# The MLP's first product, 512 columns at a time or 256

## The chip, the cores and the metric

The kernel runs on one NeuronCore of a Trainium2 chip. The metric is the device time of one execution in microseconds (us). Its engines run programs of their own and meet through semaphores: TensorE (PE in the profile, with its weight loads in a row of their own, PEld), VectorE (DVE), ScalarE (ACT), GpSimd (POOL) and SyncE (SP), which here only issues DMAs.

## The reference

Sliding-window attention over 8 batches, 8 heads, 576 positions and 64 features per head, followed by a two-layer MLP over the 4608 tokens:

```
scores = (q @ k^T) / sqrt(64) + alibi bias, masked to 0 <= i - j < 128
attn   = softmax(scores)
x      = (attn @ v), heads joined: 4608 tokens x 512
h      = x @ w_in                      # 512 -> 2048
g      = 0.5 * h * (1 + erf(h / sqrt(2)))
out    = g @ w_out                     # 2048 -> 512
```

Everything is float32 at the interface. The kernel reaches that accuracy with pairs of 16-bit numbers: a value is split into a high and a low half, and a product of two such values is the sum of three 16-bit products (high by high, low by high, high by low).

## The kernel before

**Tiles.** The 4608 tokens are nine tiles of 512, t = 0 to 8. Tile t is finished by attention over batches t and t - 1, since a batch has 576 tokens. Attention goes by units, (b, hp): a batch and one of four pairs of heads. A unit has scores (`sc`, L394), `s` with the bias (L416), a softmax into `e_main` (exponentials on ACT, the high half on POOL at L489, the low half on DVE at L143), a transposing DMA `et<-e_main` in two pieces (L492), and the product `av` with v (L529). The head pair hp of `av` becomes 128 of the 512 features of `x`: ACT writes the high half (L542), DVE the low half (`low_part`, L143).

**The MLP.** `mlp_in(t, fc)` (L566) makes one of 16 blocks of 128 features of h: 12 matrix products add up in one bank of PSUM, `ph`, named h{t}_{fc}. They go over the four groups of input features, cc (which are the head pairs of x), and for each over the three pairs of halves; the third of them reads the low half of x. The stationary operand is a 128x128 block of `wi`, and each product loads its own. A GELU on ACT (L586 in tile 0, L589 after it) empties the bank, and POOL and DVE split the result into halves (L590, L143). There are four banks for h and the output products together (tag "mm"), four for scores and av (tag "att"), and three buffers for the GELU's float32 result (tag "ob"). `mlp_out` (L601, products at L608 in tile 0 and at L611 after it) is the second layer; its 512 columns are the output features.

**Stages.** In tile 0 the weights are turned into halves on DVE and ACT while the first MLP runs; this is the time up to about 210 us, with the four units of batch 1 in its last third. From then on the loop at L721 runs through tiles 1 to 8: 16 blocks of h, then 16 groups of output products, with the scores and av of the next batch put between them. For tiles 7 and 8 there is no attention left to mix in. `split_qk(b)` (L340) takes the largest absolute value of q and of k (`stq`), makes scales from them (`scq`) and splits both into `qbuf` and `kbuf`.

**What sets the order.** The program is written in the order of these loops, and a scheduler with a model of the engines puts the instructions of each engine in the order in which its model finds them ready, priorities first. Each engine, and the queue of SP, then runs its list strictly in that order. An instruction that is not ready holds up all that stand behind it on its engine. Two calls raise priorities by 400 instructions: the exponentials (`EXP_AHEAD`), and the first product of tile 0 (L682).

Of the kernel before, what the change touches and what calls it, by code (L numbers as in the profile page):

```python
# [19 lines left out]
P = 128  # L20
# [4 lines left out]
NCC, NFC = DM // P, DFF // P  # L25
NT = B * S
TT = 512
# [25 lines left out]
def attention_gelu_mlp(  # L53
# [10 lines left out]
    nc = tc.nc  # L64
# [77 lines left out]
    def low_part(dst, src, scale, high):  # L142
        nc.vector.scalar_tensor_tensor(  # L143
            out=dst, in0=src, scalar=scale, in1=high, op0=ALU.mult, op1=ALU.subtract
        )
# [64 lines left out]
    wi, wo, zo = [], {}, []  # L210
# [68 lines left out]
    def x_tile(t):  # L279
        if t not in xt:  # L280
            xt[t] = pool.tile([P, NCC, 2, TT], F16, tag="x", name=f"x{t}", bufs=2)
        return xt[t]
# [283 lines left out]
    def mlp_in(t, fc):  # L566
        n, k = divmod(fc, 2)
        ph = psum.tile([P, TT], F32, tag="mm", name=f"h{t}_{fc}", bufs=4)
        x = x_tile(t)
        i = 0  # L570
        for cc in range(NCC):
            for a, b in ((0, 0), (1, 0), (0, 1)):
                nc.tensor.matmul(  # L573
                    ph, wi[n][:, a, cc, k * P : (k + 1) * P], x[:, cc, b, :],
                    start=(i == 0), stop=(i == 3 * NCC - 1),
                )
                i += 1
        q, r = divmod(fc, 4)
        if r == 0:
            if t == 0:  # L580
                g_of[t, q] = pool.tile([P, 4, TT], F32, tag="g", name=f"g{t}_{q}", bufs=4)
            else:
                g_of[t, q] = pool.tile([P, 4, 2, TT], F16, tag="g", name=f"g{t}_{q}", bufs=4)
        g = g_of[t, q]
        if t == 0:
            nc.scalar.activation(g[:, r], ph, AF.Gelu, scale=gsc[t, n])  # L586
            return
        g32 = pool.tile([P, TT], F32, tag="ob", name=f"g32_{t}_{fc}", bufs=3)
        nc.scalar.activation(g32, ph, AF.Gelu, scale=gsc[t, n])  # L589
        nc.gpsimd.tensor_scalar(g[:, r, 0], g32, gsg[t, n], 1.0, op0=ALU.mult, op1=ALU.mult)  # L590
        low_part(g[:, r, 1], g32, gsg[t, n], g[:, r, 0])
# [86 lines left out]
    for n in range(NWP):  # L678
        if n == 2:
            load_qk(1)  # L680
        with tc.high_priority(400):
            tile_scales(0, [n])  # L682
            for k in range(2):
                mlp_in(0, 2 * n + k)
        if n == 3:
            stat_v(1)
            split_qk(1)
            split_v(1)
            load_v(2)
        if n == 5:  # L690
            stat_v(2)
        weights_out_raw(n)
        fetch(1)
# [27 lines left out]
    for t in range(1, NTILE):  # L721
        b = t + 1
# [4 lines left out]
        for step in range(2 * NFC):  # L727
            if step < NFC:
                mlp_in(t, step)
            else:  # L730
                tb, q = divmod(step - NFC, 4)
                for fc in range(4 * q, 4 * q + 4):
                    mlp_out(t, tb, fc)
            if b >= B:
                continue
            if step in at:
                hp, i = at[step]
# [56 lines left out]
```

## Time and profile before

| | us |
|---|---|
| three runs | 956.73, 960.18, 960.32 (median 960.18) |
| the profiled execution, its own time | 963.32 |
| its span, first to last instruction | 961.4 |
| PE busy | 922.8 |
| DVE busy | 643.7 |
| ACT busy | 436.6 |
| POOL busy | 255.8 |

The profiled execution lies 3.14 us above the median of the three runs, and 1.9 us of its time lie outside the span. The durations below are those of the profiled execution. In a row of the profile, `L573 PE MATMUL h<-x,wi 128*128 128x512 f16 x1728 | 386.7, 382 | ...` reads: line 573, engine, operation, what is written from what, the part of the array, the shape of the moving operand, the count; then busy time in us and the mean duration of one in ns. Matrix products are pipelined, so that the mean duration of one (382 ns) is longer than the distance from one to the next. A row of the timeline begins with start and length in us, and ends with the idle time ahead of it and what ended it, in brackets. `A:B` rows give the busy time of each engine within a stretch, with its count of instructions, the granted share of the TensorE clock, and what the DMA engines did.

### The profile page before, as it was taken

To read this page: it belongs to the slowest core of one execution; us is meant where nothing else is said; L and a number is where in the kernel's file an instruction comes from. 1 tells how busy PE (TensorE), PEld (TensorE's weight loads), DVE (VectorE), ACT (ScalarE), POOL (GpSimd) and SP (SyncE) were. 2 spreads that over 40 slices of the span, in tenths; PEclk is the share of its full clock that TensorE was granted. 3 is DMA by queue.
4 is the path that set the end of the run, shared out by engine and by line. 5 is a ranking of instruction groups with operands and counts; after the bars stand their busy time and mean duration, and the time that the engine had idled before them with its cause. 6 is when DMAs were issued, how large, how long until landed. Compare 5 with 4: busy or idle time off the path is not lost. (4 is left out here: it accounts for less than half of the span.)

```text
span 961.4 us, 17491 instructions
## 1 busy us (share of the span) xinstructions
PE 922.8 (96%) x6996; PEld 446.1 (46%) x6996; DVE 643.7 (67%) x1270; ACT 436.6 (45%) x943; POOL 255.8 (27%) x516
## 2 busy tenths in 40 slices
PE   7988999769999899999999999999999999999998
PEld 3553444334454345444544444444544454444443
DVE  6699999989985877688767876777566632201300
ACT  6565445545553565256526653564465413201200
POOL 1010103324441433144313530363144312201200
PEclk9789999989999999999999999999999999999999
DMA  9525742972466224713372357244313430000000
GB/s 320 201 69 167 235 137 39 217 201 60 84 130 157 50 50 80 206 40 61 85 194 49 59 94 171 56 78 83 79 25 57 83 73 12 1 22 23 1 12 33
DMA packets 172451, 91.18 MB, mean 95 GB/s; under 512 B 132561, under 2 KB 153169, under 8 KB 172241
## 3 DMA queue, kind: packets, MB, share of 16 engines
q1 hardware_dynamic: 172368, 90.06, 37.9%
q8 instruction: 55, 0.90, 0.4%
q14 instruction: 28, 0.22, 0.1%
HBM read 46.53 MB, written 9.44 MB: 58 GB/s over the span
## 5 line engine op out<-in xcount | busy, mean ns | idle before, releaser
L573 PE MATMUL h<-x,wi 128*128 128x512 f16 x1728 | 386.7, 382 | 9.6 <-ACT g L589 3.9
L573 PEld LDWEIGHTS <-wi 128*128 128x128 f16 x1728 | 166.6, 98 | 212.4 <-issue 14.0
L611 PE MATMUL o<-wo,g 128*128 128x512 f16 x1152 | 259.9, 379 | 0.0
L611 PEld LDWEIGHTS <-g 128*128 128x128 f16 x1536 | 145.9, 98 | 174.3
L590 POOL TENSOR_SCALAR g<-g,sg 128x512 f16<-128x512 f32 x128 | 100.1, 786 | 288.7 <-ACT g L589 281.7
L143 DVE SCALAR_TENSOR_TENSOR g<-g,sg,g 128x512 f16<-128x512 f32 x128 | 106.2, 843 | 92.0 <-POOL g L590 92.0
L483 ACT ACTIVATE s<-s,nmax 128x192 f32<-128x192 f32 x252 | 111.2, 443 | 107.7 <-DVE nmax L480 105.0
L489 POOL TENSOR_SCALAR e_main<-s,z 128x192 f16<-128x192 f32 x252 | 124.3, 511 | 114.9 <-issue 37.3
L589 ACT ACTIVATE g<-h,gs 128x512 f32<-128x512 f32 x128 | 85.9, 687 | 137.3 <-PE h L573 108.5
L143 DVE SCALAR_TENSOR_TENSOR e_main<-s,z,e_main 128x192 f16<-128x192 f32 x252 | 112.1, 487 | 11.1 <-POOL e_main L489 10.8
L611 PE MATMUL o<-wo_first,g 128*128 128x512 f16 x384 | 88.2, 379 | 0.0
L394 PE MATMUL sc<-kbuf,qbuf 64*64 64x192 f16 (+1 forms) x1656 | 77.6, 266 | 9.4 <-DMA kbuf<-kp 4.4
L416 DVE SCALAR_TENSOR_TENSOR s<-sc,cs,bias_h 128x384 f32<-128x384 f32 x112 | 63.9, 606 | 15.1 <-PE sc L394 14.9
L542 ACT ACTIVATE x<-av,cx 128x448 f16<-128x448 f32 (+6 forms) x52 | 23.9, 477 | 86.0 <-PE av L529 85.8
L480 DVE TENSOR_REDUCE nmax<-s 128x5 f32<-128x960 f32 (+1 forms) x56 | 58.5, 1044 | 2.2
L608 PE MATMUL o<-zo,g 128*128 128x512 f32 x128 | 57.0, 598 | 0.0
L529 PE MATMUL av<-et,vbuf 128*64 128x128 f16 (+1 forms) x1680 | 45.2, 213 | 11.4 <-DMA et<-e_main 10.3
L421 POOL MEMSET s<- 64x128 f32 (+1 forms) x112 | 19.6, 176 | 134.5 <-DVE s L416 133.7
L619 ACT ACTIVATE ob<-o,so 128x512 f32<-128x512 f32 x16 | 10.9, 679 | 96.9 <-PE o L611 96.8
L394 PEld LDWEIGHTS <-qbuf 64*64 64x64 f16 x1512 | 35.2, 106 | 42.0 <-issue 39.4
L529 PEld LDWEIGHTS <-vbuf 128*64 128x64 f16 x1680 | 42.2, 113 | 21.3 <-issue 19.5
L621 DVE TENSOR_SCALAR ob<-o,so 128x512 f32<-128x512 f32 x16 | 11.9, 744 | 60.0 <-PE o L611 60.0
(128 smaller groups left out, 715.1 us busy)
## 6 DMA issues: line engine op xcount, KB each, us to landing
v<-vp SPq DMA_DIRECT2D x32, 320.0 KB, 5.0
out<-ob SPq DMA_DIRECT2D x36, 256.0 KB, 2.1
raw<-w_in SPq DMA_DIRECT2D x8, 1024.0 KB, 14.1
raw<-w_out SPq DMA_DIRECT2D x8, 1024.0 KB, 5.0
q<-qp SPq DMA_DIRECT2D x7, 1152.0 KB, 6.1
k<-kp SPq DMA_DIRECT2D x7, 1152.0 KB, 6.3
qbuf<-qp SPq DMA_DIRECT2D x4, 288.0 KB, 4.5
kbuf<-kp SPq DMA_DIRECT2D x4, 288.0 KB, 4.9
```

Of the source, the lines that this page charges most:

```text
L143: nc.vector.scalar_tensor_tensor(out=dst, in0=src, scalar=scale, in1=high, op0=ALU.mult, op1=ALU.subtract)
L394: nc.tensor.matmul(ps[bank][o, n, 0:W], a, m, start=(i == 0), stop=(i == len(terms) - 1 and b > 0), skip_group_check=True,)
L416: nc.vector.scalar_tensor_tensor(out=s[:, bank[0] : bank[0] + k, :], in0=ps[bank][:, 0:k, 0:W], scalar=cs, in1=bias.broadcast_to([P, k, W] ...
L480: nc.vector.tensor_reduce(out=nmax[:, r], in_=s[:, r], axis=AX.X, op=ALU.max, negate=True)
L483: nc.scalar.activation(s[:, i, :], s[:, i, :], AF.Exp, bias=nmax[:, i : i + 1], accum_out=z[:, i : i + 1])
L489: nc.gpsimd.tensor_scalar(e[:, i, 0, c], s[:, i], z[:, i : i + 1], 1.0, op0=ALU.mult, op1=ALU.mult)
L529: nc.tensor.matmul(av[r, (j - blocks[0]) * QB : (j - blocks[0] + len(js)) * QB], v32s[b][:, hp, kb, r] if b < EXACT else vbuf[:, vi, hp, k ...
L573: nc.tensor.matmul(ph, wi[n][:, a, cc, k * P : (k + 1) * P], x[:, cc, b, :], start=(i == 0), stop=(i == 3 * NCC - 1),)
L589: nc.scalar.activation(g32, ph, AF.Gelu, scale=gsc[t, n])
L590: nc.gpsimd.tensor_scalar(g[:, r, 0], g32, gsg[t, n], 1.0, op0=ALU.mult, op1=ALU.mult)
L608: nc.tensor.matmul(o, g[:, r, c], zo[n][:, n % 2, k * DM : (k + 1) * DM], start=(fc == 0), stop=(fc == NFC - 1))
L611: nc.tensor.matmul(o, g[:, r, a, c], wo[n][:, b, k, :], start=(fc == 0 and i == 0), stop=(fc == NFC - 1 and i == 2),)
```

## The change

Each block of features of h is now made in two halves of 256 tokens. First 12 products fill the left half of the bank, then 12 more, with the same 12 stationary blocks loaded again, fill the right half. The GELU still reads the whole bank at once. `skip_group_check=True` tells the checker that two accumulations live in a bank.

```
-        i = 0
-        for cc in range(NCC):
-            for a, b in ((0, 0), (1, 0), (0, 1)):
-                nc.tensor.matmul(
-                    ph, wi[n][:, a, cc, k * P : (k + 1) * P], x[:, cc, b, :],
-                    start=(i == 0), stop=(i == 3 * NCC - 1),
-                )
-                i += 1
+        for c in (slice(0, TT // 2), slice(TT // 2, TT)):
+            i = 0
+            for cc in range(NCC):
+                for a, b in ((0, 0), (1, 0), (0, 1)):
+                    nc.tensor.matmul(
+                        ph[:, c], wi[n][:, a, cc, k * P : (k + 1) * P], x[:, cc, b, c],
+                        start=(i == 0), stop=(i == 3 * NCC - 1), skip_group_check=True,
+                    )
+                    i += 1
```

The 1728 products of L573 and their 1728 weight loads become 3456 of each (at L574). Later lines move down by one. Because the scheduler counts and models instructions, the lists of the other engines change too. From tile 2 on DVE, ACT, POOL and SP differ only by neighbours that change places; the larger differences lie in tile 0 and at the start of tile 1. PE differs also at the openings of tiles 2 and 3, in the same way as shown here for tile 1: the last av of tile 2 has nine half products of h_0 ahead of it in place of nine whole ones.

**PE, the opening of tile 1.** The blocks h_0 to h_3 of tile 1 are worked on while the last head pairs of batch 1 come in. Before, at the point where the low half of the last head pair's x is there, one product of each of the four blocks is left (`sc_0` are scores of batch 2):

```order
L394 MATMUL sc_0_2_2171<-kbuf,qbuf 64x192
L573 LDWEIGHTS wi_635
L573 MATMUL h_0_1970<-x_1107,wi_635 128x512
L573 LDWEIGHTS wi_635
L573 MATMUL h_1_1988<-x_1107,wi_635 128x512
L573 LDWEIGHTS wi_638
L573 MATMUL h_2_2016<-x_1107,wi_638 128x512
L573 LDWEIGHTS wi_638
L573 MATMUL h_3_2033<-x_1107,wi_638 128x512
L394 LDWEIGHTS qbuf
L394 MATMUL sc_0_4_2217<-kbuf,qbuf 64x192
```

Now, at the same point, h_0 goes on from its left half into its right half; the list has 13 products of h_0 here, then 13 of h_1, of h_2 and of h_3, and then h_4:

```order
L394 MATMUL sc_0_2_2471<-kbuf,qbuf 64x192
L574 LDWEIGHTS wi_635
L574 MATMUL h_0_2162<-x_1299,wi_635 128x256
L574 LDWEIGHTS wi_635
L574 MATMUL h_0_2162<-x_1299,wi_635 128x256
```

In the whole list no right half begins ahead of the end of its left half. So 44 of the 48 products of 512 columns stood ahead of this point, and now 44 of the 96 of 256 columns do.

**SP, the transposing DMAs of batch 1's units** (`et_1` to `et_3` are the units hp 1 to 3, two pieces each; `k_2` is the k of batch 2, `wo_first` a copy of a weight tile). Before:

```order
L492 DMA_TRANSPOSE et_1_1288<-e_main 128x20x128
L622 DMA out<-ob_0_1830 128x512
L273 DMA wo_first<-wo_1735 128x4096
L622 DMA out<-ob_2_1838 128x512
L492 DMA_TRANSPOSE et_1_1288<-e_main 128x16x128
L492 DMA_TRANSPOSE et_2_1415<-e_main 128x20x128
L622 DMA out<-ob_1_1834 128x512
L622 DMA out<-ob_3_1842 128x512
L337 DMA k_2_1930<-kp 128x4x576
L492 DMA_TRANSPOSE et_2_1415<-e_main 128x16x128
L492 DMA_TRANSPOSE et_3_1611<-e_main 128x20x128
```

Now:

```order
L492 DMA_TRANSPOSE et_1_1480<-e_main 128x20x128
L492 DMA_TRANSPOSE et_1_1480<-e_main 128x16x128
L492 DMA_TRANSPOSE et_2_1607<-e_main 128x20x128
L623 DMA out<-ob_0_2022 128x512
L623 DMA out<-ob_1_2026 128x512
L623 DMA out<-ob_2_2030 128x512
L273 DMA wo_first<-wo_1927 128x4096
L623 DMA out<-ob_3_2034 128x512
L492 DMA_TRANSPOSE et_2_1607<-e_main 128x16x128
L337 DMA k_2_2122<-kp 128x4x576
L492 DMA_TRANSPOSE et_3_1803<-e_main 128x20x128
```

The second piece of et_1 and the first of et_2 have moved ahead of the weight copy, and the load of k_2 behind the second piece of et_2.

**DVE, the end of unit (1, 3).** Before, the maximum of k_2 (`stq`) stands between the fourth and the fifth of the nine low halves of `e_main` of this unit:

```order
L143 SCALAR_TENSOR_TENSOR e_main<-s_3_1540,z_3_1610,e_main 128x192 x2
L208 TENSOR_REDUCE stq_1933<-k_2_1930 128x1
L143 SCALAR_TENSOR_TENSOR e_main<-s_3_1540,z_3_1610,e_main 128x192 x2
L113 COPY quarters<-stq_1933 32x2
L143 SCALAR_TENSOR_TENSOR e_main<-s_3_1540,z_3_1610,e_main 128x192
```

Now it stands behind all nine of them, and behind the low half of x of head pair 2:

```order
L143 SCALAR_TENSOR_TENSOR e_main<-s_3_1732,z_3_1802,e_main 128x192 x3
L143 SCALAR_TENSOR_TENSOR x_1299<-av_2_1_1940,cx_1_979,x_1299 128x448
L143 SCALAR_TENSOR_TENSOR e_main<-s_3_1732,z_3_1802,e_main 128x192
L143 SCALAR_TENSOR_TENSOR x_1721<-av_2_2_1985,cx_2_1155,x_1721 128x128
L208 TENSOR_REDUCE stq_2125<-k_2_2122 128x1
```

The steps behind it are in the same order as before: the scales, `qbuf`, `kbuf`, and only then the low half of x of head pair 3.

## The prediction

> **What bounds the kernel now.** I read the page's busy shares first, then busy time by stretches, then PE's timeline where it has gaps.
>
> ```profile
> PE 922.8 (96%) x6996; PEld 446.1 (46%) x6996; DVE 643.7 (67%) x1270; ACT 436.6 (45%) x943; POOL 255.8 (27%) x516
> L573 PE MATMUL h<-x,wi 128*128 128x512 f16 x1728 | 386.7, 382 | 9.6 <-ACT g L589 3.9
> L573 PEld LDWEIGHTS <-wi 128*128 128x128 f16 x1728 | 166.6, 98 | 212.4 <-issue 14.0
> ...
> core 0: us, PE busy (x) PEld busy (x) DVE busy (x) ACT busy (x) POOL busy (x), PEclk, DMA share, GB/s
> 60.00:130.00 70.00, 66.00 (x289) 30.78 (x288) 69.54 (x97) 35.37 (x42) 7.31 (x4) 1.00 0.55 178
> ...
> 195.00:200.00 5.00, 4.20 (x70) 3.31 (x71) 4.93 (x14) 1.00 (x2) 1.82 (x4) 0.50 0.39 65
> ...
> 215.00:250.00 35.00, 35.00 (x228) 15.84 (x227) 33.95 (x77) 19.23 (x37) 15.77 (x26) 1.00 0.32 69
> ```
>
> PE is busy for 96% of the span, but not everywhere alone: from 60 to 130 us DVE is full (69.54 of 70 us) and PE is not. From 215 us on PE has no idle time (35.00 of 35), and after that it only stops for a few waits. So an addition to h's products in tile 0 should vanish behind DVE, and one in tiles 1 to 8 should count in full. What matters is the distance between products, not the 382 ns that one lasts.
>
> **What a half product costs.** The rows are of PE's timeline (a run in tile 7, a run of float32 products, a run of av) and PEld's:
>
> ```profile
> 819.76 8.58 PE L573 MATMUL h<-x,wi 128*128 128x512 f16 x39
> ...
> 819.98 8.08 PEld L573 LDWEIGHTS <-wi 128*128 128x128 f16 x38
> ...
> 110.70 19.48 PE L608 MATMUL o<-zo,g 128*128 128x512 f32 x45
> ...
> 494.81 0.78 PEld L529 LDWEIGHTS <-vbuf 128*64 128x64 f16 x26
> ...
> L529 PEld LDWEIGHTS <-vbuf 128*64 128x64 f16 x1680 | 42.2, 113 | 21.3 <-issue 19.5
> L608 PE MATMUL o<-zo,g 128*128 128x512 f32 x128 | 57.0, 598 | 0.0
> ```
>
> 39 products take 8.58 us with the last one's 0.38 us: (8.58 - 0.38) / 38 = 215.8 ns apart. The float32 products of the same shape are (19.48 - 0.60) / 44 = 429.1 ns apart, twice as long within 2.5 ns. If float32 streams its columns twice, then columns cost 213.3 ns per 512 and each product a fixed 2.5 ns. A product of 256 columns then takes 106.7 + 2.5 = 109.1 ns, a pair 218.3, which is **2.5 ns more for each old product**. The bounds: 0 if the 2.5 ns goes with columns, and the whole weight load of 98 ns if the load no longer hides. A load starts with the product ahead of it (the run of loads begins one distance, 0.22 us, into the run of products). It has 109 ns for 98. And in av, 26 loads, 13 for each half of the array's columns, run in 0.78 us, one each 56 ns or so, though a load's row says 113 ns. So the load's duration isn't its pace, and I take 2.5 ns. A rule of the Trainium skill speaks against it: "TensorE: Matmul & The Clock Gate", Part 3 (Packing small matmuls, The mechanism), says that weight loads overlap products in flight only when they go to other rows of the array. By that rule 1728 more loads would stand on the path. The trace disagrees: the 38 loads above go to the same 128 rows as the products among which they run, and the products are no further apart for it.
>
> In tiles 2 to 8 there are 7 x 16 x 12 = 1344 old products: 1344 x 2.5 ns = **+3.3 us**, all on PE's path. Tile 0's 192 would add 0.5 us, which lies behind DVE. GELUs also change places with other work of ACT in tile 0. One example is h_9's GELU, now behind a weight step that waits for its DMA. I price that at nothing, because PE has waits enough behind it, the next rows.
>
> **The opening of tile 1.** This is PE's timeline from the end of batch 1's scores, then DVE's and SP's around it:
>
> ```profile
> 178.46 0.69 PE L394 MATMUL sc<-kbuf,qbuf 64*64 64x192 f16 x23 [3.43 <-DVE s L416]
> ...
> 188.32 2.75 PE L573 MATMUL h<-x,wi 128*128 128x512 f16 x12 [1.80 <-ACT x L542]
> 195.72 2.77 PE L529 MATMUL av<-et,vbuf 128*64 128x128 f16 x66 [4.64 <-DMA et<-e_main]
> 198.57 3.47 PE L573 MATMUL h<-x,wi 128*128 128x512 f16 x12
> 205.26 1.60 PE L529 MATMUL av<-et,vbuf 128*64 128x128 f16 x66 [3.22 <-DMA et<-e_main]
> ...
> 209.81 1.02 PE L573 MATMUL h<-x,wi 128*128 128x512 f16 x4
> ...
> 211.78 7.93 PE L573 MATMUL h<-x,wi 128*128 128x512 f16 x36 [0.58 <-ACT g L589]
> ...
> 190.71 0.57 DVE L143 SCALAR_TENSOR_TENSOR e_main<-s,z,e_main 128x192 f16<-128x192 f32 x1 [0.62 <-POOL e_main L489]
> ...
> 193.78 2.55 DVE L208 TENSOR_REDUCE stq<-k 128x1 f32<-128x2304 f32 x1 [1.01 <-DMA k<-kp]
> ...
> 204.01 2.62 DVE L143 SCALAR_TENSOR_TENSOR qbuf<-q,scq,qbuf 128x2304 f16<-128x2304 f32 x1 [2.17 <-ACT qbuf L351]
> 206.55 2.61 DVE L143 SCALAR_TENSOR_TENSOR kbuf<-k,scq,kbuf 128x2304 f16<-128x2304 f32 x1
> 209.08 0.68 DVE L143 SCALAR_TENSOR_TENSOR x<-av,cx,x 128x448 f16<-128x448 f32 x1
> ...
> 187.16 0.39 SPq L337 DMA_DIRECT2D k<-kp  x1
> ```
>
> PE waits here again and again for the last head pairs, and fills the time with 44 of the 48 products of h_0 to h_3. The last 4 start at 209.81, when the low half of the last x is there (DVE, 209.08 + 0.68). Call that time T. From T on PE works without a stop but for 0.58 us in which it waits for the first GELU to free a bank.
>
> Now a right half cannot begin ahead of its left half's end, so only 44 of 96 half products stand ahead of T, 4.8 us of cover where 9.5 were. Left behind T: before, 4 + 12 x 12 = 148 products, 31.9 us; now 52 + 12 x 24 = 340 half products, 37.1 us. That is 5.2 us more. The 0.58 us go, because 48 half products run while the first GELU works. **+4.6 us**, if T stays. This has tile 1's own 2.5 ns per product in it.
>
> Does T stay? T hangs on DVE's list: maximum of k_2, scales, `qbuf`, `kbuf`, x. Two things move. k_2's DMA was issued at 187.16 and is now issued behind et_2's second piece; its landing, waited for at 193.78, gets later. But the last five low halves of `e_main` no longer stand behind the maximum, so et_3 and the last av get earlier, and less is left for DVE behind the maximum. Earlier than DVE's idle time allows T cannot be: 0.62 + 1.01 + 2.17 = 3.8 us. Later, I give it 4 us, somewhat more than the 3.22 us that the last av waited for its transposition, as the only DMA wait here of that kind. Between these ends I take 0.
>
> **The opening of tile 2** has the same form once more:
>
> ```profile
> 295.81 2.10 PE L573 MATMUL h<-x,wi 128*128 128x512 f16 x9
> 298.38 1.55 PE L529 MATMUL av<-et,vbuf 128*64 128x128 f16 x54 [0.47 <-DMA et<-e_main]
> ...
> 300.07 0.62 DVE L143 SCALAR_TENSOR_TENSOR x<-av,cx,x 128x384 f16<-128x384 f32 x1 [2.46 <-ACT x L542]
> ...
> 323.58 2.75 PE L573 MATMUL h<-x,wi 128*128 128x512 f16 x12 [0.25 <-ACT g L589]
> 328.76 7.03 PE L573 MATMUL h<-x,wi 128*128 128x512 f16 x24 [2.43 <-ACT g L589]
> ...
> PE h L573 <- ACT g L589: 3.9, 4, 2.4
> PE av L529 <- DVE g L143: 1.2, 1, 1.2
> ...
> 594.06 1.60 PE L529 MATMUL av<-et,vbuf 128*64 128x128 f16 x66 [1.71 <-DMA et<-e_main]
> ```
>
> Nine products of h_0 cover the wait for the last transposition; nine half products cover 9 x 106.7 ns = **1.0 us** less, and the wait grows by that. Behind that av, 18 half products (2.0 us) still cover the 0.8 us until x is there (its low half ends on DVE at 300.07 + 0.62, 0.8 us after the av's end at 298.38 + 1.55). From tile 3 on the last av has output products ahead of it, which don't change. PE's short wait of 0.25 us for a GELU at 323.58 goes for the most part, since the blocks ahead of it are each 12 x 2.5 = 30 ns longer: **-0.2 us**.
>
> **The sum** is 4.6 + 1.0 + 3.3 - 0.2 = +8.7 us, from 963.32 to 972.0 us for an execution like the profiled one. That one lies 3.14 us above the median of the three runs, 960.18, and so I forecast **968.9 us**. About 0.5%, or 4.8 us, is what a measurement of this kernel can tell from no change.
>
> **The rivals.**
> *The lateness is taken up downstream (not slower).* PE still waits 0.25, 2.43, 0.61 and 1.71 us for GELUs and a transposition in tiles 2 to 5 and 1.18 us for DVE (the rows above; 0.61 is what remains of the 3.9 us for GELUs). If those waits end when ACT and DVE are ready by their own pace, a late PE loses them: 8.7 - 6.2 = +2.5 us, 962.7. It decides where ACT starts its GELUs at 328: no later than before, or 6 us later with PE. For it: DVE is 33.95 of 35 us busy in tile 1. Against it: PE is 35.00 of 35, and the exponentials that delay those GELUs wait for scores that PE makes. Chance 0.12.
> *T comes early.* All 3.8 us of DVE's idle time go: +4.9, 965.1. Chance 0.15.
> *T comes late, or the clock drops.* From 195 to 200 us the granted clock was 0.50, after PE's wait of 4.64 us, and 12 products took 3.47 us in place of 2.75. With less cover PE idles longer just ahead of T, and a drop of 3.4 us behind T costs 1.7 us; with T 4 us late this gives up to +14.4, 974.6 us. Chance 0.14. The same page of the Trainium skill (Part 1) says that a whole idle window of some 3.4 us halves the clock; the trace agrees, with 4.64 us idle ahead of the stretch at 0.50.
> *Weight loads stop hiding.* 1728 x 98 ns = +169 us, 1130 us. The av row speaks against it: 0.03.
> *T and ACT's new order in tile 0 both help, and it gets faster:* nothing in the rows gives 5 us. 0.03.
> The forecast itself has 0.53.
>
> **Range and chances.** The forecast with T off by 2 us and the fixed cost between 0 and 2.5 ns spans about 964 to 972. The early and late cases and the taken-up lateness widen it to **962 to 975 us**. Slower by over 0.5% (above 965.0): the forecast, the late case, the loads, and half of the early case, about 0.77. Within 0.5%: 0.20. Faster: 0.03.
>
> **What would show it.** In the profile of the changed kernel, runs of half products stand 109 ns apart (107.9 or 120 would refute the 2.5 ns). The products of h_0 to h_3 behind T number 52, and PE waits for the last transposition of tile 2 about 1.4 us where it waited 0.47. From tile 3 on each tile is 0.5 us longer. The forecast is wrong if T moves by more than 3 us, if ACT's GELUs at 328 stay in place while PE comes late, or if the instruction queue can't feed twice as many loads and products, which would show as gaps in tiles 7 and 8, where nothing else runs.

## The result, and the profile after

The changed kernel took 970.42 us (median of four runs: 968.28, 970.41, 970.44, 978.09), the kernel before beside it 960.25 (956.73 to 960.97): a ratio of 1.0125, with a 95% interval from 1.0079 to 1.0171. The forecast was 968.9, slower by over 0.5%. The sum is close, but two of its terms were wrong in opposite directions, and the two profiles alone don't show it.

The page of the changed kernel, with the lines that answer to the first three of the prediction:

```profile
PE 927.7 (96%) x8724; PEld 616.9 (64%) x8724; DVE 646.3 (67%) x1270; ACT 437.6 (45%) x943; POOL 253.4 (26%) x516
L574 PE MATMUL h<-x,wi 128*128 128x256 f16 x3456 | 394.3, 276 | 11.2 <-DVE x L143 3.6
L574 PEld LDWEIGHTS <-wi 128*128 128x128 f16 x3456 | 338.6, 99 | 61.0 <-issue 10.9
```

Twice as many products keep PE busy for 7.6 us more (394.3 against 386.7), and PE's idle time in front of h's products is 11.2 us where it was 9.6. One run of half products in tile 7, from the timelines of PE and of PEld:

```profile
811.74 20.47 PE L574 MATMUL h<-x,wi 128*128 128x256 f16 x186
...
811.96 20.07 PEld L574 LDWEIGHTS <-wi 128*128 128x128 f16 x184
```

186 products in 20.47 us, the last one's 0.28 taken off, are (20.47 - 0.28) / 185 = 109.1 ns apart. The loads, 99 ns long by their row, start 109 ns apart among them. That is the forecast's figure.

Next, PE's timeline of the changed kernel at the three places where a tile's h products begin (tiles 0, 1, 2), and DVE's row that ends at T:

```profile
58.02 1.05 PE L574 MATMUL h<-x,wi 128*128 128x256 f16 x8
...
184.34 1.48 PE L574 MATMUL h<-x,wi 128*128 128x256 f16 x12
188.16 1.47 PE L574 MATMUL h<-x,wi 128*128 128x256 f16 x12 [2.34 <-ACT x L542]
191.85 2.77 PE L529 MATMUL av<-et,vbuf 128*64 128x128 f16 x66 [2.21 <-DMA et<-e_main]
194.71 2.25 PE L574 MATMUL h<-x,wi 128*128 128x256 f16 x12
201.91 2.77 PE L529 MATMUL av<-et,vbuf 128*64 128x128 f16 x66 [4.95 <-DMA et<-e_main]
...
210.29 15.98 PE L574 MATMUL h<-x,wi 128*128 128x256 f16 x131
...
301.98 1.15 PE L574 MATMUL h<-x,wi 128*128 128x256 f16 x9
303.90 1.55 PE L529 MATMUL av<-et,vbuf 128*64 128x128 f16 x54 [0.77 <-DMA et<-e_main]
...
209.37 0.68 DVE L143 SCALAR_TENSOR_TENSOR x<-av,cx,x 128x448 f16<-128x448 f32 x1
```

T is at 209.37 + 0.68 = 210.05 us, against 209.76 before. It looks as if T had stayed, as forecast. But the row at the top has its partner in the kernel before at 63.19 us (quoted further down). This execution came to tile 0 5.2 us earlier, through code that the change doesn't touch. Its granted clock over the first 57.7 us was 0.97, that of the kernel before 0.84. Measured from that row, T is 5.5 us later. The first row of each kernel's tile 0 differs from run to run, from 57.8 to 71.1 us in the 14 profiles of this study. So in what follows times are counted between four points: A, the first h product of tile 0; T; B, the first h product of tile 2; and the end of PE's last product. A to tile 1 is from A to the first h product of tile 1. "Own time" is the profiled execution's, "median" that of all timed runs beside their own runs of the kernel before, and "more" the 95% interval of the ratio less one, in per cent. One of the ten runs with h_4 to h_15 took 2385 us; the interval leaves it out.

| half products in | A to tile 1 | A to T | T to B | B to end | own time | median | more |
|---|---|---|---|---|---|---|---|
| none (before) | 115.9 | 146.6 | 86.1 | 661.8 | 963.32 | 960.25 | |
| all (after) | 126.3 | 152.0 | 91.9 | 662.9 | 970.44 | 970.42 | 0.79 to 1.71 |
| all, again | 125.6 | 150.7 | 92.1 | 660.5 | 974.08 | 974.44 | 1.02 to 2.08 |
| tiles 0, 1 | 125.8 | 150.8 | 90.5 | 658.8 | 971.05 | 972.66 | 1.12 to 1.79 |
| tile 0 | 125.0 | 151.2 | 88.9 | 658.4 | 968.04 | 970.04 | 0.73 to 1.55 |
| tile 0, h_0 to h_3 | 124.5 | 150.8 | 88.2 | 658.8 | 967.04 | 967.68 | 0.40 to 1.61 |
| tile 0, h_4 to h_15 | 118.1 | 149.0 | 87.4 | 659.9 | 959.65 | 965.08 | 0.07 to 0.74 |
| all but h_0 to h_3 of 1 to 3 | 126.0 | 152.5 | 86.6 | 661.1 | 969.80 | 971.37 | 0.85 to 1.55 |
| all but h_0 to h_3 of 0 to 3 | 118.4 | 149.1 | 87.3 | 661.8 | 961.68 | 969.81 | 0.67 to 1.29 |
| all, interleaved | 117.7 | 149.9 | 87.5 | 661.9 | 968.28 | 970.34 | 0.69 to 1.50 |
| tiles 1 to 8 | 116.5 | 149.4 | 91.2 | 663.0 | 972.78 | 970.65 | 0.66 to 1.74 |
| tile 1 | 116.1 | 147.3 | 91.7 | 660.3 | 968.48 | 967.95 | 0.41 to 1.05 |
| tiles 2 to 8 | 116.1 | 146.7 | 86.2 | 660.9 | 970.37 | 964.57 | 0.25 to 0.78 |
| quarters in 7, 8 | 116.0 | 146.9 | 85.8 | 662.8 | 966.37 | 966.37 (one) | |

### The profile page after: what moved, and what is told of

Its sections match the earlier page's. It is cut to its first block, busy times and chain, and to the rows that moved or that the text cites. A ratio compares the mean times of both kernels' runs of the same rounds, so it can differ in the third digit from the quotient of the medians.

```text
span 968.7 us, 20945 instructions
## 1 busy us (share of the span) xinstructions
PE 927.7 (96%) x8724; PEld 616.9 (64%) x8724; DVE 646.3 (67%) x1270; ACT 437.6 (45%) x943; POOL 253.4 (26%) x516
## 4 chain that ended last, share of the span: by engine, by line
PE 68%; DVE 15%; DMA 6%; ACT 4%; issue 3%; SPq 1%; POOL 1%; DVEq 0%; ACTq 0%; POOLq 0%
PE o L612 32%; PE h L574 27%; PE sc L394 4%; PE av L529 4%; DMA v<-vp 2%; DVE e_main L143 1%; DVE stv L208 1%; DVE s L416 1%; ACT s L483 1%; DVE nmax L480 1%; SPq L298 1%; DVE vbuf L143 1%; DVE zo L190 1%; DMA raw<-w_out 1%; DVE stq L208 1%
## 5 line engine op out<-in xcount | busy, mean ns | idle before, releaser
L574 PE MATMUL h<-x,wi 128*128 128x256 f16 x3456 | 394.3, 276 | 11.2 <-DVE x L143 3.6
L574 PEld LDWEIGHTS <-wi 128*128 128x128 f16 x3456 | 338.6, 99 | 61.0 <-issue 10.9
L489 POOL TENSOR_SCALAR e_main<-s,z 128x192 f16<-128x192 f32 x252 | 124.5, 511 | 111.0 <-issue 39.4
L590 ACT ACTIVATE g<-h,gs 128x512 f32<-128x512 f32 x128 | 86.6, 687 | 145.6 <-PE h L574 123.1
L143 DVE SCALAR_TENSOR_TENSOR e_main<-s,z,e_main 128x192 f16<-128x192 f32 x252 | 113.2, 493 | 13.5 <-POOL e_main L489 13.3
L612 PE MATMUL o<-wo_first,g 128*128 128x512 f16 x384 | 88.2, 379 | 0.0
L394 PE MATMUL sc<-kbuf,qbuf 64*64 64x192 f16 (+1 forms) x1656 | 75.0, 265 | 11.6 <-ACT qbuf L331 4.5
```

The costliest lines, as they stand in the source:

```text
L143: nc.vector.scalar_tensor_tensor(out=dst, in0=src, scalar=scale, in1=high, op0=ALU.mult, op1=ALU.subtract)
L394: nc.tensor.matmul(ps[bank][o, n, 0:W], a, m, start=(i == 0), stop=(i == len(terms) - 1 and b > 0), skip_group_check=True,)
L489: nc.gpsimd.tensor_scalar(e[:, i, 0, c], s[:, i], z[:, i : i + 1], 1.0, op0=ALU.mult, op1=ALU.mult)
L574: nc.tensor.matmul(ph[:, c], wi[n][:, a, cc, k * P : (k + 1) * P], x[:, cc, b, c], start=(i == 0), stop=(i == 3 * NCC - 1), skip_group_che ...
L612: nc.tensor.matmul(o, g[:, r, a, c], wo[n][:, b, k, :], start=(fc == 0 and i == 0), stop=(fc == NFC - 1 and i == 2),)
```

## The experiments

The edit of nearly all is the loop over halves with a condition (`parts`); the medians of the kernel before in the three groups of runs were 959.95, 960.63 and 959.91 us.

```
-        for c in (slice(0, TT // 2), slice(TT // 2, TT)):
+        parts = 2 if t < 2 else 1
+        for c in [slice(p * TT // parts, (p + 1) * TT // parts) for p in range(parts)]:
```

**Half products in tiles 0 and 1 only** (the lines above).

> Half products in tiles 0 and 1 only, whole products in tiles 2 to 8. Theory of the opening (fewer products ahead of T, the moment at which the low half of the last x of tile 1 is there): the 4.6 us of the prediction's sum stay, and up to 1.7 us that the half clock behind T took in the changed kernel's profile; of these, waits downstream in tiles 4 and 5 (1.71 and 1.18 us before) may take up 0 to 2.9 us. So 962 to 966.5 us against 960.25, and tile 2's h products begin 4.6 to 6.3 us later than before. Rival (the fixed 2.5 ns per product is nearly all of the loss, the opening little): 16 x 12 x 2.5 ns = 0.5 us, so 960 to 961 us.

972.66 us, above the upper end. Tile 2's h products begin at 306.65, 10.8 us later than in the profile before, not 4.6 to 6.3. T to B is 4.5 us longer, as the theory of the opening has it, but A to T is 4.2 us longer too, and 2.1 us are a later start of tile 0.

**Half products in tiles 2 to 8 only** (`parts = 2 if t >= 2 else 1`).

> Whole products in tiles 0 and 1, half products in tiles 2 to 8. Theory: 1344 x 2.5 ns = 3.3 us, and 0.3 to 1.0 us at the opening of tile 2, of which tile 4's and 5's waits (1.71 and 1.18 us before) take up 0 to 2.9 us: 961 to 964.6 us, h of tile 2 beginning where it did before (295.8, within 1 us), each of tiles 6, 7, 8 longer by 0.48 us. Rival (the opening of tile 1 is not the cause, the half products are): this kernel is as slow as the changed one, about 969 to 970 us. The rival that lateness costs nothing downstream: 960 to 961.5 us.

964.57 us, at the upper end of the theory. The profiled execution reached tile 0 late (71.10), so B is not where it was, but A to T and T to B are those of before within 0.2 us. From B to the end it took no longer than before, though 1344 products are in halves. So the 4.6 us by which the median is higher aren't in these stretches.

**Left and right product of each block of `wi` side by side.** In this kernel the two accumulations of a bank run into one another, so that its sums aren't the reference's; the number, the form and the order of the products, and the loads, are as described.

```
         i = 0
         for cc in range(NCC):
             for a, b in ((0, 0), (1, 0), (0, 1)):
+                for c in (slice(0, TT // 2), slice(TT // 2, TT)):
...
```

> All products are half products as in the changed kernel, but the left and right product of each block of wi stand one behind the other, so a right half no longer waits for its left half's end and 88 of the 96 half products of h_0 to h_3 of tile 1 can stand ahead of T, as 44 of 48 whole ones before. Theory of the opening: behind T stand 8 + 288 = 296 half products, 32.3 us against 31.9, so +0.4 us there and +3.3 us in tiles 2 to 8, less 0 to 2.9 us taken up downstream: 961 to 964.5 us. Rival (the loss comes with the number of products, wherever they stand): about 969 to 970 us. A further rival, that a second product on the same weights is cheaper because its load is left out: products less than 109 ns apart, 960 to 961 us.

970.34 us, the rival's number. The profiled stretches don't show the rival's reason: they are 3.3 us (A to T) and 1.4 us (T to B) above before, where the changed kernel has 4.1 to 5.5 and 5.9 to 6.0. But they make only 4.8 of the median's 10.4 us, so the rival isn't refuted here. The loads are all there (3456), and products stay 109 ns apart.

**Whole products in h_0 to h_3 of tiles 1 to 3** (`parts = 1 if 1 <= t <= 3 and fc < 4 else 2`).

> The changed kernel with whole products in h_0 to h_3 of tiles 1 to 3, so the cover ahead of T is that of before (44 of 48 whole products), and half products everywhere else. Theory of the opening: behind T stand 4 whole and 288 half products, 32.3 us, +0.4 us; tiles 2 to 8 have 1344 - 96 = 1248 old products in halves, +3.1 us; less 0 to 2.9 us taken up downstream: 961 to 964 us, and tile 2's h products begin within 1 us of before's 295.8. Rival (the loss comes with the number of products): 968 to 970 us.

971.37 us: a miss in the time. But T to B is 86.6 us, 0.5 above before and 5.4 below the changed kernel. The opening of tile 1 had been repaired, and the loss stood elsewhere: A to T is 152.5. The kernels so far with left halves first in tile 0 have 126 us from A to tile 1, the others 116 to 118. That was the new theory, and the next group of runs took it up.

**Whole products in tile 0** (`parts = 2 if t >= 1 else 1`).

> The changed kernel with whole products in tile 0; half products in tiles 1 to 8. New theory (after the first four runs: kernels with half products in tile 0, left half first, take 126 us from the first h product of tile 0 to the first of tile 1, the others 116 to 118): tile 0 gives the greater part of the loss. Then here that stretch is 116 us again, the time from T to tile 2's first h product stays 4.6 to 6 us longer than before's, tiles 2 to 8 cost 3.3 us and waits downstream take back up to 3 us: 963 to 967 us, 4 to 7 us faster than the changed kernel. Rival (the old theory, tile 1's opening and the half products are the loss, tile 0 none): 969 to 971 us.

970.65 us with a wide interval: the rival's number, 3.8 us below the changed kernel beside it. The stretches are the theory's (116.5, and T to B is 5.1 us longer), but T is 2.8 us late: the maximum of k_2 begins 1.2 us later behind A, and between it and T DVE waits 1.80 us for a high half from POOL.

**Half products in tile 0 only** (`parts = 2 if t == 0 else 1`).

> Half products in tile 0 only. New theory (tile 0): 126 us from the first h product of tile 0 to that of tile 1, T 4 to 6 us later behind tile 0's first product than before, and tiles 1 to 8 as before, less what waits downstream take up (0 to 3 us): 962 to 967 us. Rival (the old theory: 0.5 us that lie behind DVE): 960 us, within 1 us of before.

970.04 us: the forecast's "0.5 us, which lies behind DVE" is refuted by this run alone. It is even above the new theory's range. T to B is 2.8 us longer too, though tile 1 is whole: 20 more of the score products (0.72 us in the kernel before) stand behind T, and the granted clock in the 5 us behind T is 0.75 (before 1.00), which is 1.25 us. The rest isn't traced.

**Half products in tile 1 only** (`parts = 2 if t == 1 else 1`).

> Half products in tile 1 only. Old theory's term alone: the time from T to tile 2's first h product grows by 4.6 us (up to 6 with the half clock behind T), waits downstream take back 0 to 3 us: 962 to 966 us, and 116 us in tile 0's stretch. Rival (tile 0 is the whole loss, as the restored openings of tile 1 in the kernels with interleaved and with whole first blocks brought nothing to the time): 960 to 961 us.

967.95 us, 0.41 to 1.05% more and 2 us above the range; T to B is 5.7 us longer, and A to tile 1 is that of before. So tile 1's opening costs what the forecast said or more, apart from tile 0. The single costs don't add up: tile 0 alone 9.4, tile 1 alone 7.3, tiles 2 to 8 alone 4.6 us, together 21, and all three at once 10 to 14. By the profiled stretches from A to the end they are 4.1, 4.8 and -0.7, together 8.2, and all at once 12.4 and 8.9.

**The changed kernel again.**

> The changed kernel once more, beside the three others on one chip. Every theory: 968 to 972 us. Its profile shows what varies from run to run: the start of tile 0's first h product (58.0 us in the first profile, 63 to 71 in the others) and the stretches at half clock. New theory: 126 us from tile 0's first h product to tile 1's whatever the start. Rival (that stretch is long only where the start was early, as DVE sets the end): 120 us or less if tile 0 starts at 63 us.

974.44 us, 2.4 above the range. Its profile starts tile 0 2.0 us later than before's, and has the long stretch nevertheless (PE, then DVE):

```profile
65.22 1.05 PE L574 MATMUL h<-x,wi 128*128 128x256 f16 x8
...
190.78 1.48 PE L574 MATMUL h<-x,wi 128*128 128x256 f16 x12
...
307.99 1.15 PE L574 MATMUL h<-x,wi 128*128 128x256 f16 x9
...
215.23 0.68 DVE L143 SCALAR_TENSOR_TENSOR x<-av,cx,x 128x448 f16<-128x448 f32 x1
```

190.78 - 65.22 = 125.6, and T at 215.91, 150.7 behind A. The rival is out: it isn't the early start.

**Which half products of tile 0: h_4 to h_15, or h_0 to h_3** (`parts = 2 if t == 0 and fc >= 4 else 1`, and `fc < 4`).

> Half products in tile 0 only, and there only in h_4 to h_15; whole ones in h_0 to h_3 and in tiles 1 to 8. Theory of the order (with left halves first in h_0 to h_3 of tile 0, ACT is given two steps of w_out's preparation ahead of its first two GELUs, and DVE and PE follow late): ACT's order is that of before at that place here, the stretch from tile 0's first h product to tile 1's is 116 to 118.5 us, T stands 146.5 to 150 us behind tile 0's first h product, 960 to 963 us. Rival (any half products in tile 0 do it): 124 to 126 us, T 150.5 to 152.5 us, 968 to 971 us as with all of tile 0 in halves.

> Half products in h_0 to h_3 of tile 0 alone, 96 products in the place of 48; all others whole. Theory of the order: 124 to 126 us from tile 0's first h product to tile 1's, T 150.5 to 152.5 us behind it, 966 to 971 us. Rival (the number of half products in tile 0 counts): 116 to 118 us, T 146.5 to 148 us, 960 to 961 us.

965.08 us (2 above the theory's range) and 967.68 (within it), 118.1 and 124.5 from A to tile 1, T 149.0 and 150.8 behind A. The 48 old products of h_0 to h_3 give 8.6 of the 9.1 us by which the stretch is longer with all of tile 0 in halves; the 144 of h_4 to h_15 alone give 2.2. What happens is seen in three timelines. The kernel before (PE, ACT, DVE):

```profile
63.19 1.90 PE L573 MATMUL h<-x,wi 128*128 128x512 f16 x8
...
73.91 3.83 PE L573 MATMUL h<-x,wi 128*128 128x512 f16 x17 [1.38 <-DVE x L143]
...
89.98 20.88 PE L573 MATMUL h<-x,wi 128*128 128x512 f16 x96 [1.06 <-ACT g L586]
...
74.86 1.27 ACT L586 ACTIVATE g<-h,gs 128x512 f32<-128x512 f32 x2
76.01 2.20 ACT L184 ACTIVATE zo<-raw 128x1024 f32<-128x1024 f32 x2
...
89.27 2.40 ACT L586 ACTIVATE g<-h,gs 128x512 f32<-128x512 f32 x4
...
88.19 0.32 DVE L556 TENSOR_SCALAR gs<-pww,pwv 128x1 f32<-128x1 f32 x2
...
90.89 2.53 DVE L208 TENSOR_REDUCE stq<-q 128x1 f32<-128x2304 f32 x1
```

The kernel with half products in h_0 to h_3 of tile 0 alone:

```profile
63.62 1.05 PE L575 MATMUL h<-x,wi 128*128 128x256 f16 x8
...
73.12 5.51 PE L575 MATMUL h<-x,wi 128*128 128x256 f16 x49 [2.93 <-DVE x L143]
...
95.10 22.57 PE L575 MATMUL h<-x,wi 128*128 128x512 f16 x96 [3.00 <-ACT g L588]
...
75.49 2.23 ACT L184 ACTIVATE zo<-raw 128x1024 f32<-128x1024 f32 x2 [1.52 <-issue]
...
79.03 1.27 ACT L588 ACTIVATE g<-h,gs 128x512 f32<-128x512 f32 x2
...
94.36 2.42 ACT L588 ACTIVATE g<-h,gs 128x512 f32<-128x512 f32 x4 [3.44 <-DVE gs L556]
...
91.05 2.56 DVE L208 TENSOR_REDUCE stq<-q 128x1 f32<-128x2304 f32 x1
...
94.10 0.22 DVE L556 TENSOR_SCALAR gs<-pww,pwv 128x1 f32<-128x1 f32 x1
```

Eight half products of a block are done ahead of the last x instead of eight whole ones, so PE waits 2.93 us for x's low half where it waited 1.38. The scheduler's lists now have two steps of the weights (`zo`) ahead of the first GELUs on ACT, and on DVE the maximum of q (2.56 us) ahead of the scales `gs` of the next GELUs. ACT waits 3.44 us for that scale, and PE waits 3.00 us for a bank where it waited 1.06. The last 96 products begin 31.5 us behind A where it was 26.8, and are slower, which the windows of the two kernels show (columns: window, then PE, PEld, DVE, ACT, POOL busy, then granted clock, DMA share, GB/s):

```profile
95.00:100.00 5.00, 4.90 (x15) 1.89 (x15) 5.00 (x10) 2.81 (x6) 0.00 (x0) 0.66 0.33 91
```

```profile
95.00:100.00 5.00, 5.00 (x25) 2.29 (x24) 5.00 (x8) 3.00 (x4) 0.00 (x0) 1.00 0.34 91
```

The clock was 0.66 after the 3.00 us of idling; before (second row) it was full. The 96 products took 22.57 us for 20.88. By their end PE is 6.4 of the 8.6 us behind; the rest isn't traced. In all 14 profiles the order on ACT goes with the length: the six with the two `zo` steps ahead of the first GELUs have 124.5 to 126.3 us from A to tile 1, the eight with the GELUs first 115.9 to 118.4. No run changes the order alone.

What DVE does meanwhile is seen in windows. The kernel before, from A to 170 us and from there to T, and the changed kernel again, in stretches of the same place:

```profile
63.19:170.00 106.81, 103.27 (x494) 47.36 (x492) 106.28 (x173) 52.53 (x82) 18.07 (x27) 1.00 0.46 144
170.00:209.76 39.76, 26.21 (x405) 15.30 (x404) 35.31 (x77) 19.50 (x50) 11.15 (x29) 0.87 0.82 185
```

```profile
65.22:172.03 106.81, 98.51 (x670) 64.29 (x668) 105.72 (x173) 51.47 (x81) 15.78 (x26) 0.98 0.45 138
172.03:215.91 43.88, 29.42 (x420) 19.84 (x419) 37.34 (x77) 21.05 (x51) 12.24 (x30) 0.81 0.76 169
```

DVE is full in both for the first 106.81 us, as the forecast said, while PE is busy for 4.8 us less (98.51 for 103.27). In the last stretch DVE has 2.0 us more to do (37.34 for 35.31) and stands idle for 6.54 us instead of 4.45. That is the 4.1 us of T. Why its 77 instructions there take longer than the 77 before isn't settled; some work may have come over from the first stretch, which has 0.56 us less.

T itself hangs on the maximum of k_2. The load of k_2 now stands on SP behind the second piece of et_2, and the maximum on DVE behind all low halves of `e_main`. In the changed kernel's first profile (the rows of before, at 187.16 and 193.78, stand in the prediction):

```profile
184.46 5.44 SPq L492 DMA_TRANSPOSE et<-e_main  x1
190.00 0.52 SPq L337 DMA_DIRECT2D k<-kp  x1
...
196.59 2.55 DVE L208 TENSOR_REDUCE stq<-k 128x1 f32<-128x2304 f32 x1 [0.63 <-DMA k<-kp]
```

The load goes out 132.0 us behind A, before it was 124.0. In both kernels DVE waits for its landing (0.63 and 1.01 us) and begins the maximum 6.6 us after the load goes out. From there to T it takes 13.5 us instead of 16.0, because the five low halves have left that place: 8.0 - 2.5 = 5.5 us, which is all by which T is later. The changed kernel again has 6.6 - 2.5. An earlier load alone would have gained no more than the 0.63 us, for the work ahead of the maximum ends no sooner; in the kernels with halves in tile 0 alone, and in its h_0 to h_3 alone, DVE waits 2.4 and 2.3 us for it. All nine profiles with any half products in tile 0 have the load behind that piece, 128.1 to 132.0 us behind A, and T at 149.0 to 152.5. The five with a whole tile 0 have it ahead of the piece, at 124.0 to 125.0, and T at 146.6 to 149.4. No run moved the load alone.

**Whole products in h_0 to h_3 of tiles 0 to 3, halves elsewhere** (`parts = 1 if t <= 3 and fc < 4 else 2`).

> Whole products in h_0 to h_3 of tiles 0 to 3, half products in all other blocks (1536 of 1728 old products). Theory of the two openings (tile 0's order and tile 1's cover are the loss, half products elsewhere cost 2.5 ns each): 116 to 118.5 us from tile 0's first h product to tile 1's, T 146.5 to 150 us behind the first, tile 2's first h product 86 to 87.5 us behind T, the rest 660 to 662.5 us: 961 to 966 us. Rival (half products cost wherever they stand): 968 us or more.

All four stretches came out in or at the edge of what was expected: 118.4, 149.1, 87.3 and 661.8. The time did not: 969.81. The profiled execution's own time, 961.68, is what the theory expects, but it lies 8 us under the median. A good part of that can be an early start: it came to tile 0 at 57.97, 5.2 us earlier than before's, with a granted clock of 0.97 over the first 57.7 us. Counted from A to the end it took 898.1 us, 3.7 more than before. Of its twelve executions three took 961.7 to 964.8 us and nine 969.1 to 972.4; what those nine lose is in no trace. So both openings are repaired in the trace but for 2.5 us at T, and still the time stands 0.67 to 1.29% above before. This is the miss that stays open.

**Quarter products in tiles 7 and 8** (`parts = 4 if t >= 7 else 1`), where no other work runs.

> Tiles 7 and 8 with four products of 128 columns for each old product, all else whole as before. Theory of a fixed 2.5 ns for each product: four take 4 x (53.3 + 2.5) = 223.3 ns where one took 215.8, so from tile 7's first h product to tile 8's 82.88 + 192 x 0.0075 = 84.3 us, and 84.5 from there to the end. Rival (a weight load of 98 ns becomes the pace as soon as a product is shorter): 4 x 98 = 392 ns, 116.7 us for each tile.

From tile 7 to tile 8 it took 84.32 us, from there to the end 84.48: the fixed cost, to 0.02 us. PE's and PEld's timeline:

```profile
794.78 7.42 PE L575 MATMUL h<-x,wi 128*128 128x128 f16 x130
...
794.95 7.13 PEld L575 LDWEIGHTS <-wi 128*128 128x128 f16 x127
```

Products of 128 columns, each with a weight load, are (7.42 - 0.22) / 129 = 55.8 ns apart (0.219 us is the mean of one in its group), that is 53.3 + 2.5.

## Why the prediction was right, and where it was wrong

**A fixed 2.5 ns for each product, loads hidden: right.** 109.1 ns at 256 columns, 55.8 at 128. Tiles 6, 7 and 8 each take 0.48 us longer, 192 x 2.5 ns, in every kernel that has them in halves (97.38, 83.36 and 83.52 us against 96.90, 82.88 and 83.04).

**Less cover at the opening of tile 1: right.** 4.6 us were forecast, and 340 half products of h stand behind T where 148 whole ones stood, as forecast. T to B grew by 5.9 and 6.0 us in the two profiles of the changed kernel and by 5.7 with tile 1 alone in halves; with h_0 to h_3 of tiles 1 to 3 whole and all else in halves the growth is 0.5. The rest came as the rival on the clock had it, at its small end: in the changed kernel the first window behind T has a clock of 0.66, before it had 1.00.

```profile
210.00:215.00 5.00, 5.00 (x41) 3.67 (x34) 5.00 (x6) 1.67 (x2) 0.40 (x2) 0.66 1.04 392
```

```profile
210.00:215.00 5.00, 4.42 (x25) 1.97 (x24) 4.70 (x5) 2.87 (x4) 2.90 (x5) 1.00 1.05 388
```

5 x 0.34 = 1.7 us of work are lost there. In the five profiles with all of tile 1 in halves, one half behind the other, the clock over the 5 us behind T was 0.95, 0.83, 0.69, 0.66 and 0.63, and T to B grew by 4.5, 5.1, 5.7, 5.9 and 6.0 us: 4.1 to 4.2 us in each, once the lost clock is taken off. PE had idled for 4.95 us ahead of the row of 201.91 above, and the clock was 0.50 from 200 to 210 us. The Trainium skill, "TensorE: Matmul & The Clock Gate", Part 1, has the clock halved after an idle window of some 3.4 us; the 4.95 us agree with it. In tile 0 a wait of 3.00 us, shorter than that, was enough: the clock behind it was 0.66 over 5 us. There the trace differs, and it decides.

**Tile 0 for nothing: wrong, and this is the step that failed.** "GELUs also change places with other work of ACT in tile 0 [...] I price that at nothing, because PE has waits enough behind it". The waits behind were not slack: half products in h_0 to h_3 of tile 0 alone make the way to tile 1 8.6 us longer, move T by 4.2 us, and cost 0.40 to 1.61%. The term for T failed too ("Between these ends I take 0"): measured from A, T is 4.1 to 5.5 us later. The forecast had named both movers, the load of k_2 and the five low halves, but they don't cancel: the maximum behind that load begins 6.6 to 8.0 us later, and the low halves give back 2.5. By the prediction's own mark (T moves by more than 3 us) the reasoning is wrong there.

**Lateness taken up downstream: held to be a rival, partly true.** For everything behind B, 3.3 + 1.0 - 0.2 = 4.1 us were forecast. The seven profiles with halves in the later tiles have 660.5 to 663.0 us from B to the end, mean 661.7, six with whole ones there, the kernel before among them, 658.4 to 661.8, mean 659.7: 2.0 us, of which tiles 6 to 8 make 1.4. (The run with quarters is left out of both.) PE's waits from 216 us on, in the views of before, after, and after again:

```profile
PE h L573 <- ACT g L589: 3.3, 3, 2.4
PE av L529 <- DMA et<-e_main: 2.2, 2, 1.7
PE av L529 <- DVE g L143: 1.2, 1, 1.2
```

```profile
PE h L574 <- ACT g L590: 3.5, 2, 2.4
PE av L529 <- DMA et<-e_main: 0.8, 1, 0.8
PE sc L394 <- DVE s L416: 0.3, 1, 0.3
```

```profile
PE h L574 <- ACT g L590: 2.3, 2, 1.4
PE av L529 <- DMA et<-e_main: 1.3, 2, 0.8
PE sc L394 <- DVE s L416: 0.2, 1, 0.2
```

6.7 us of waiting became 4.6 and 3.8: a late PE finds the transposition of tile 4 (in the second profile all but 0.52 us) and DVE's g of tile 5 done. The wait of 2.4 for the GELUs stayed in one profile, though, so that the rival's full 6.2 us don't hold either. In the other it was 0.87, and the clock behind it stayed at 1.00, where the first has 0.66 over 5 us (1.7 us): with the 0.8 us of other waiting that is the difference of 2.4 us between the two behind B. The opening of tile 2 cost 0.3 us (a wait of 0.77 for 0.47) where 1.0 was forecast.

**The sum.** By stretches, the mean of the two changed profiles against before: A to T +4.8 (forecast 0), T to B +6.0 (4.6), B to the end -0.1 (4.1); together 10.7 where 8.7 was forecast. So that 968.9 came close to 970.42 is partly luck: a cost of 4 to 5 us at tile 0 and T that was priced at nothing stood against 4 us that were forecast behind B and did not come, 2.1 to 2.9 of them because waits were taken up.

**What stays open.** In all changed kernels that were timed more than once, but for the first run of the change, the median lies further from before than the stretches from A to the end do, by 1 to 7 us. The one profile of the kernel before is 3 us above its median, and what of that it lost behind A is missing from each difference. The kernel with quarters, which has no other products than before's up to tile 7, took 1.8 us less from A to there; that is one execution against another. The start of tile 0 is in the medians and not in the stretches: the three profiles that came to it at 57.8 to 58.0 us had a granted clock of 0.97 up to there, the one that came at 71.1 had 0.70 over the same 57.7 us. How often each kernel starts early is not traced. So it isn't shown whether half products away from the openings cost more than 2.5 ns each. Their number alone is not it: 1344 old products in tiles 2 to 8 cost 4.6 us by the median, the 48 of h_0 to h_3 of tile 0 cost 7.8. Nor is it shown why single costs of 9.4, 7.3 and 4.6 us add up to 10 to 14.

## What to carry to other kernels

Splitting a product costs little in itself; the order of the parts can cost much. Where an input comes late, parts that finish one behind the other halve the work that can be done ahead of it, and a scheduler then fills the other engines with other things: keep the first blocks whole, and follow each swapped instruction, transfers on the DMA queue included, to who waits for it before pricing it at nothing. To compare two profiles, count from an event that both have behind the stretch that varies, not from the start; a milestone that "stays" may have moved by the very amount by which the start differed.

## What was unexpected of the hardware

A weight load of 128 columns has a duration of 98 ns in its row, and yet a pair of load and product keeps up one each 55.8 ns, with loads into the same 128 rows as the products in flight. The rule cited in the prediction ("TensorE: Matmul & The Clock Gate" of the Trainium skill, Part 3) would forbid that; the trace decides against it here too.

A start of accumulation in the right half of a bank, put between the first and the second product of the left half, spoiled the sums, while halves one after the other, each with its own start, leave them whole. The Trainium skill, "PSUM — Partial Sum Buffer" (The four PSUM rules), says that the second start clears the marks of the first group in the same bank; the run agrees as far as its sums differ from the reference; which terms were lost isn't shown.
